# Cluster assignment of two attention halves through one bank and one argmax, with a reordered slot softmax and a new instruction order

## The chip, the cores and the metric

The kernel runs on one core of a Trainium2 chip. A core has TensorE (PE, which loads a stationary operand and streams a moving one against it), VectorE (DVE), ScalarE (ACT), GpSimd (POOL), and SyncE (SP), whose queue issues most of the DMAs. The metric is the device time of one launch in microseconds (us), taken as a median over runs.

## The reference

Two batches, eight heads, 768 tokens of 64 numbers. Each query and key token goes to the nearest of 16 centroids by a cosine, and a query attends only to keys of its own cluster. The result, 1536 tokens of 512, goes through a soft mixture of eight experts with four slots each, and then through a normed, gated feed-forward layer.

```python
q_assign = np.argmax(np.einsum('bhsd,hcd->bhsc', q_n, c_n), axis=-1)
k_assign = np.argmax(np.einsum('bhsd,hcd->bhsc', k_n, c_n), axis=-1)
mask = q_assign[:, :, :, None] == k_assign[:, :, None, :]
scores = np.where(mask, scale * np.matmul(q, k.transpose(0, 1, 3, 2)), -1e9)
x = softmax(scores) @ v                         # 1536 x 512
...
logits = x @ phi                                # 1536 x 32
slot_input = softmax(logits, axis=0).T @ x      # 32 x 512
slot_out[e] = np.maximum(slot_input[e] @ w1[e], 0.0) @ w2[e]    # 512 -> 1024 -> 512
y = softmax(logits, axis=1) @ slot_out          # 1536 x 512
...
xn = y / rms * rms_g
g = xn @ w_gate
out = (silu(g) * (xn @ w_val)) @ w_out          # 512 -> 1536 -> 512
```

## The kernel before

The program is written as operations (`Sched.op`), each with an engine or a choice of engines and a cost, the operations it depends on, and a sort key. A list scheduler in Python then fixes the order on every engine ahead of the build: of the operations whose inputs and buffers are free it takes the one with the least start time plus penalty. A table of constants at the head of the file (`KO`, an offset to the key for each operation's name, and some forty single numbers such as `SH`, `KS`, `AP`) feeds those keys and penalties. Buffers come from rings with fixed counts; `ms` is a ring of one PSUM bank, `big` one of three pairs of banks, `P` one of seven tiles in SBUF.

**Attention.** Eight pairs of heads, each made ready by `prepare(i)` and then worked off by two of the sixteen `unit`s. `prepare` loads q, k and v, and for each of the two halves of 384 tokens (`half(g)`) turns them on PE (L358), copies them to SBUF, multiplies them with the centroids (`cluster`, L395), copies the scores (`cevac`, tile cs), turns them again (`clusterT`, three transposes, L406) into a bank sc, adds the two partial scores of each (`part`, two reductions, L412) and finds the cluster with five passes of 192 numbers a partition (`argmax`, L436 to L445: maximum, difference, index where equal, maximum, one-hot E). Three transposes of E (`onehot`, L456) and three copies by ACT (`oq` L459, `ok` twice, L465) put the one-hot rows under q and k, where they act as the mask inside the score product. The chain of a half holds the one `ms` bank at several points, and it stands in DVE's queue among the score maxima of a unit.

A unit takes 768 keys by 768 queries in six blocks: `s1` (L526) multiplies scores once to find each row's maximum (`s1max`, DVE, L538), `mrow` puts the negated maxima (nr) where the second product can subtract them, `s2` (L578, L580) multiplies scores again, `exp` (ACT, L587) makes the weights P, `acc` (POOL or DVE, L242) adds the blocks of P for the sum, and `av` (L604) multiplies P with v. Then `lT` and `lgt` (L638, L644) make the sums and the slot logits, `oT` (L681) turns the output os. In the last unit the sums are made by `sums(0)` over acc and `sums(1)` over the last block of P (L661), in products whose moving operand is one column of ones.

**Slot softmax, experts, gates.** `middle` makes the slot softmax of the second batch: maximum (L1101 to L1110), exponentials, slot input si (L1181), its transposes (L1203, L1209) and the scaled slot input SITz (L1213), which the first expert product h (L1322) needs. The softmax of the other axis is `csm` (seven steps, L1233 to L1246, of which four on DVE come after the sum's exponential). The expert weights w come by SP's queue (L928, L930) in loads of 512 KB; the ring of w buffers comes free as the products h (L1322) and h2 (L1348) end. Of the loads in SP's queue one waits for the last logit sum L (L717). `cols` (L1363) turns an expert's result into columns of eight. Then `gates`: a Gram matrix (L1420), twelve products cq for the norm (L1448), the gate and value matrices of the 32 slots (gp, L1538), their casts and differences Gh and Gst (L234, L1571), the transposed slot weights cc (cT, L1291), and the loop over 36 blocks with g and v (L1652), the gate function sg (L1660), hh and hl, and the output products o (L1692). `warm` is a number of products that nobody reads (W3 to W8, WA0 to WA2, on PE).

## Time and profile before

| | us |
|---|---|
| runs: lowest, median, highest | 494.28, 494.79, 495.96 |
| profiled execution, its own time | 493.6 |
| span of the profile | 491.9 |
| PE busy | 456.6 (93%) |
| DVE busy | 321.7 (65%) |
| ACT busy | 279.2 (57%) |
| POOL busy | 216.5 (44%) |

The profile is of one execution. "Busy" counts the time in which an engine works on data. The clock column gives the share of full speed that PE's throttle granted, the two levels being 1.2 and 2.4 GHz (0.50 and 1.00). "Idle before" names what ended the idle time of an engine. By stage, the span is about: start to 36 us, attention to 292, slot softmax to 302, experts to 351, the way to the first gate product to 365, gates to 487, and a tail of output copies.

### The profile page before, as it was taken

To read this page: it belongs to the slowest core of one execution; us is meant where nothing else is said; L and a number is where in the kernel's file an instruction comes from. 1 tells how busy PE (TensorE), PEld (TensorE's weight loads), DVE (VectorE), ACT (ScalarE), POOL (GpSimd) and SP (SyncE) were. 2 spreads that over 40 slices of the span, in tenths; PEclk is the share of its full clock that TensorE was granted. 3 is DMA by queue.
4 is the path that set the end of the run, shared out by engine and by line. 5 is a ranking of instruction groups with operands and counts; after the bars stand their busy time and mean duration, and the time that the engine had idled before them with its cause. 6 is when DMAs were issued, how large, how long until landed. Compare 5 with 4: busy or idle time off the path is not lost. (4 is left out here: it accounts for less than half of the span.)

```text
span 491.9 us, 7819 instructions
## 1 busy us (share of the span) xinstructions
PE 456.6 (93%) x2794; PEld 330.3 (67%) x2794; DVE 321.7 (65%) x640; ACT 279.2 (57%) x582; POOL 216.5 (44%) x149
## 2 busy tenths in 40 slices
PE   6889998999999999899889998989989999999995
PEld 5766775777768756667667673335528878888884
DVE  6776889799999899788996143021157894444440
ACT  5568585876877866887756602231066664334332
POOL 2319767674877859484738800012025660000000
PEclk9889998999999999999999978999889999999999
DMA  6455415523634345746236949999502402002002
GB/s 173 117 154 171 115 41 151 135 65 97 198 112 150 94 134 171 200 155 190 98 121 227 339 170 362 378 398 392 225 0 90 168 1 87 0 1 85 0 1 85
DMA packets 30822, 71.96 MB, mean 146 GB/s; under 512 B 4064, under 2 KB 10304, under 8 KB 30784
## 3 DMA queue, kind: packets, MB, share of 16 engines
q1 hardware_dynamic: 26080, 55.73, 34.3%
q10 hardware_dynamic: 4704, 15.73, 10.1%
q8 instruction: 22, 0.36, 0.3%
q14 instruction: 16, 0.13, 0.1%
HBM read 61.97 MB, written 3.15 MB: 132 GB/s over the span
## 5 line engine op out<-in xcount | busy, mean ns | idle before, releaser
L242 POOL TENSOR_TENSOR acc<-acc,P 128x768 f32<-128x768 f32 x62 | 119.3, 1925 | 13.9 <-ACT P L587 10.5
L538 DVE TENSOR_REDUCE nm<-s 128x1 f32<-128x768 f32 x96 | 87.3, 948 | 12.5 <-PE s L526 12.0
L587 ACT ACTIVATE P<-s 128x768 f32<-128x768 f32 x96 | 75.3, 812 | 35.3 <-PE s L580 29.5
L1692 PE MATMUL o<-W,hh 128*128 128x512 f32 x288 | 89.9, 393 | 0.1
L578 PE MATMUL s<-q,k 128*128 128x384 f32 x192 | 70.0, 364 | 2.6 <-DVE nm L538 1.3
L604 PE MATMUL o<-P,rawv 128*64 128x384 f32 x384 | 67.8, 494 | 0.0
L580 PE MATMUL s<-q,k 97*128 97x384 f32 x192 | 65.7, 342 | 0.0
L1692 PEld LDWEIGHTS o<-W,hh 128*128 128x128 f32 x288 | 54.1, 188 | 12.5 <-POOL W L242 0.5
L526 PE MATMUL s<-k,q 96*128 96x384 f32 x192 | 52.4, 369 | 5.3 <-DVE nm L538 4.3
L1692 PE MATMUL o<-W,hl 128*128 128x512 f32 x144 | 56.6, 393 | 0.4 <-DVE hl L242 0.4
L242 POOL TENSOR_TENSOR acc<-P,P 128x768 f32<-128x768 f32 x16 | 30.0, 1875 | 46.3 <-ACT P L587 46.3
L578 PEld LDWEIGHTS s<-q,k 128*128 128x128 f32 x192 | 37.2, 194 | 11.4 <-DVE nm L538 3.4
L604 PEld LDWEIGHTS o<-P,rawv 128*64 128x64 f32 x384 | 25.3, 136 | 28.7 <-issue 27.2
L1664 DVE TENSOR_TENSOR hf<-v,sg 128x512 f32<-128x512 f32 x36 | 24.7, 689 | 28.6 <-ACT sg L1660 27.6
L526 PEld LDWEIGHTS s<-k,q 96*128 96x128 f32 x192 | 31.2, 190 | 16.1 <-DVE nm L538 9.9
L580 PEld LDWEIGHTS s<-q,k 97*128 97x128 f32 x192 | 37.2, 194 | 0.0
L1660 ACT ACTIVATE sg<-g 128x512 f32<-128x512 f32 x36 | 21.4, 597 | 27.7 <-PE g L1652 27.5
L234 ACT CAST hh<-hf 128x512 fp32r<-128x512 f32 x36 | 22.3, 621 | 21.9 <-DVE hf L1664 17.8
L242 DVE TENSOR_TENSOR hl<-hf,hh 128x512 fp32r<-128x512 f32 x29 | 21.2, 731 | 17.0 <-ACT hh L234 16.0
L1692 PEld LDWEIGHTS o<-W,hl 128*128 128x128 f32 x144 | 27.0, 188 | 6.9 <-DVE hl L242 0.8
L242 POOL TENSOR_TENSOR tokk<-rawk,tokk 128x384 fp32r<-128x384 f32 x15 | 16.4, 1092 | 33.3 <-DVE tokk L236 17.6
L676 ACT ACTIVATE pl<-pl 128x128 f32<-128x128 f32 x90 | 23.6, 262 | 7.8 <-PE pl L644 4.0
(261 smaller groups left out, 760.1 us busy)
## 6 DMA issues: line engine op xcount, KB each, us to landing
w<-in_moe_w_dram SPq DMA_DIRECT2D x56, 512.0 KB
gate<-in_moe_w_gate_dram ACTq DMA_DIRECT2D x12, 512.0 KB
val<-in_moe_w_val_dram ACTq DMA_DIRECT2D x12, 512.0 KB
out<-in_moe_w_out_dram SPq DMA_DIRECT2D x10, 512.0 KB
rawk<-in_k_dram SPq DMA_DIRECT2D x8, 384.0 KB
rawq<-in_q_dram SPq DMA_DIRECT2D x8, 384.0 KB
rawv<-in_v_dram SPq DMA_DIRECT2D x8, 384.0 KB
k<-k SPq DMA_DIRECT2D x16, 192.0 KB
```

Source lines behind the costliest of these rows:

```text
L234: nc.scalar.copy(out, in_)
L242: (nc.vector if e == "dve" else nc.gpsimd).tensor_tensor(out, a, b, op=op)
L526: nc.tensor.matmul(ps[:, g, :HQ], T[q2][0:96, h, qb : qb + 128], T[f"k2_{i}_{g}"][0:96, h, :], start=True, stop=True,)
L538: nc.vector.tensor_reduce(T[f"nm{u}"][:, n : n + 1], T[f"s1_{u}{h}{j}"][:, :, :HQ], op=ALU.max, axis=AX.XY, negate=True)
L578: nc.tensor.matmul(ps[:, h, :HQ], T[f"k1_{i}_{g}"][:, h, kb], T[q1][:, h, :], start=True, stop=False)
L580: nc.tensor.matmul(ps[:, h, :HQ], T[f"k2_{i}_{g}"][0:97, h, kb], T[q2][0:97, h, :], start=False, stop=True)
L587: nc.scalar.activation(p, T[f"s2_{u}_{c}"][:, :, :HQ], AF.Exp, scale=float(1.0 / D**0.5))
L604: nc.tensor.matmul(T[f"o{u}"][64 * h : 64 * h + 64, :HQ], T[f"rawv{i}"][:, h, c, :], T[f"P{u}_{c}"][:, h, :], start=(c == 0), stop=(c == N ...
L676: nc.scalar.activation(p, p, AF.Copy, accum_out=ls_()[:, h, j : j + 1])
L1660: nc.scalar.activation(self.tile(f"sg{tg}_{f}", [128, 512], F32, "sg", "outp", 2), T[f"g{tg}_{f}"], AF.Silu)
L1664: nc.vector.tensor_tensor(self.tile(f"hf{tg}_{f}", [128, 512], F32, "hf", "outp", 2), T[f"v{tg}_{f}"], T[f"sg{tg}_{f}"], op=ALU.mult)
L1692: nc.tensor.matmul(T[f"o{tg}{q}"], T[f"{x}{tg}_{f}"][:, ts], T[f"W{f // 6}"][:, w, f % 6, :], start=(f == 0 and n == 0), stop=(f == 11 and ...
```

## The change

It has five parts.

1. The two halves of a pair share one bank sc, one tile of copied scores cs and one argmax. Transposes and the two reductions of `part` are replaced by a product of cs with a constant `fold` (128 x 64, built once by one DVE reduction), which turns the scores and adds the parts in one go. `argmax` runs once a pair over 384 numbers a partition, `onehot` is one bank of six transposes, and six row copies on ACT follow in a row. The rings cs, csb and amb go; the first half's warm products at the start go too.
2. In unit 15 the sums are products with 64 equal columns of ones, `sums(1)` comes after the last av, and the row sums are read from two banks. All its `acc` run on DVE.
3. In `middle` the step of `csm` that follows the exponential comes after SITz is issued.
4. `cols` makes 64 columns (the same eight, eight times) rather than eight; eight warm products follow the last `cols` (W9), and the other warm counts grow (W3 6 to 9, W4 20 to 30, W5 3 to 8, W6 15 to 20, W8 6 to 10).
5. The table of constants is another one, so the order on every engine is another one.

```diff
-SH = 6.48
+SH = 7.03
...
-    "oT": -20.92, "s1": -0.82, "lT": 1.82, "split_hi": 67.65, "osb": 5.16, "mag": 19.15, "guard": 7.48,
+    "oT": -35.85, "s1": -0.08, "lT": 3.19, "split_hi": 83.82, "osb": 6.03, "mag": 31.37, "guard": 7.48,
...
-        cs=1, csb=1, am=1, amb=1, E=1, nm=2, nr=1, P=PR, acc=2, os=1, l=2,
+        am=1, E=1, nm=2, nr=1, P=PR, acc=2, os=1, l=2,
...
-            def clusterT(e):
-                pt = self.bank(f"sc{i}{g}", ms)
-                for j in range(3):
-                    at = slice(j * 128, (j + 1) * 128)
-                    nc.tensor.transpose(pt[:, 128 + j * 128 :][:, :128], T[f"cs{i}{g}"][:, at], K["id"])
-            def part(e):
-                pt = T[f"sc{i}{g}"]
-                for a, b in ((0, 128), (128, 192)):
-                    nc.vector.tensor_reduce(pt[:, a:b].rearrange("p (m c) -> p m c", c=C),
...
+        def both():
+            def clusterT(g):
+                def fn(e):
+                    if g == 0:
+                        self.bank(f"sc{i}")
+                    for j in range(3):
+                        nc.tensor.matmul(T[f"sc{i}"][:, 192 * g + 64 * j :][:, :64], T[f"cs{i}"][:, g, j * 128 : (j + 1) * 128],
+                                         K["fold"], start=True, stop=True)
+                return fn
+            CS = (cv[0], "P")
+            zg = z + DG
+            p = op({"pe": 700}, clusterT(0), key=zg - 10.25, alloc=("ms",), deps=cv, uses=[CS], after=self.lastE)
+            SC = (p, "ms")
+            p = op({"pe": 700}, clusterT(1), key=zg - 10.2, uses=[CS, SC])
...
-                    v = T[f"sc{i}{g}"][:, :192].rearrange("p (m c) -> p m c", c=C)
+                    v = T[f"sc{i}"][:, :384].rearrange("p (m c) -> p m c", c=C)
...
-            p = op({"pe": 200}, onehot, key=zg - 9, deps=[a], alloc=(ms,))
+            p = op({"pe": 400}, onehot, key=zg - 9, deps=[a], alloc=("ms",))
...
-                ac.append(op({"pool": 1885, "dve": (900, 900, AP)} if u < 15 or c < 4 else {"dve": 900}, acc(c), key=zu + c + 1.6,
+                ac.append(op({"pool": 1885, "dve": (900, 900, AP)} if u < 15 else {"dve": 900}, acc(c), key=zu + c + 1.6,
...
-                    nc.tensor.matmul(pt[:, 1, HQ + 64 + 2 * n + k : HQ + 65 + 2 * n + k], x, K["ones"], start=True, stop=True)
+                    nc.tensor.matmul(pt[:, k, 64 * n : 64 * n + 64], x, K["ones"].to_broadcast([128, 64]), start=True, stop=True)
...
-            pv[-1].after.append(op({"pe": 1340}, sums(1), key=ze - 10, uses=[(ex[-1], "P"), (p, "big")]))
+            last = op({"pe": 1340}, sums(1), key=ze - 10, uses=[(ex[-1], "P"), (p, "big")], after=pv[-1:])
...
+    K["fold"] = early.tile([128, 64], F32, name="fold_")
+    nc.vector.tensor_reduce(K["fold"].rearrange("p (m c) -> p m c", c=C),
+                            K["id"].rearrange("p (m t c) -> p m c t", t=2, c=C), op=ALU.add, axis=AX.X)
...
-            a = op({"act" if k == 2 else "dve": d}, csm(k), deps=[a], key=k0 + 2 + 0.1 * k)
+            a = op({"act" if k == 2 else "dve": d}, csm(k), deps=[a], key=k0 + 2 + 0.1 * k,
+                   after=[self.slots] if k == 3 else ())
...
-                    nc.tensor.matmul(ps[:, 8 * c : 8 * c + 8], T[f"H2s{ep}"][:, c * 128 : (c + 1) * 128],
-                                     T["F8"].rearrange("p x s -> p (x s)"), start=True, stop=True)
+                    nc.tensor.matmul(ps[:, 64 * c : 64 * c + 64].rearrange("p (r n) -> p r n", n=8), T[f"H2s{ep}"][:, c * 128 : (c + 1) * 128],
+                                     T["F8"].rearrange("p x s -> p (x s)").unsqueeze(1).to_broadcast([128, 8, 8]),
+                                     start=True, stop=True)
...
+            if ep == 3:
+                self.warm(W9, [c], kk + 6.17)
```

What the order does at three places. On PE, at the end of unit 15 (P_2 to P_5 are its last blocks of weights, o its output, acc the added blocks, os the copied halves of the output, phi the slot matrix, po a turned output), before:

```order
L604 MATMUL o_3333<-P_3_3310,rawv_2850 64x384 x2
L604 MATMUL o_3333<-P_4_3316,rawv_2850 64x384 x2
L661 MATMUL pl_3358<-ones,acc_3281 128x1 x6
L661 MATMUL pl_3358<-ones,P_5_3331 128x1 x6
L681 MATMUL po_3384<-idr,os_3288 128x128 x3
L604 MATMUL o_3333<-P_5_3331,rawv_2850 64x384 x2
L644 MATMUL pl_3358<-phi,os_3392 128x64 x3
L681 MATMUL po_3405<-idr,os_3392 128x128 x3
```

and after:

```order
L619 MATMUL o_3217<-P_2_3172,rawv_2746 64x384 x2
L675 MATMUL pl_3226<-ones,acc_3156 128x64 x6
L695 MATMUL po_3244<-idr,os_3165 128x128 x3
L619 MATMUL o_3217<-P_3_3182,rawv_2746 64x384 x2
L619 MATMUL o_3217<-P_4_3189,rawv_2746 64x384 x2
L619 MATMUL o_3217<-P_5_3206,rawv_2746 64x384 x2
L675 MATMUL pl_3226<-ones,P_5_3206 128x64 x6
L659 MATMUL pl_3226<-phi,os_3269 128x64 x3
L695 MATMUL po_3283<-idr,os_3269 128x128 x3
```

The sums over acc and the turning of the first os move ahead of the av products of P_3, and the sums over P_5 behind the last av products. So the last logits (phi, os) now come six products of sums after the av product that makes their os, and not right behind it.

On DVE, from the copy of the slot input SIs to the first work of the experts (L1233 to L1246 before are the steps of the other softmax; rd is the reciprocal of the slot sums), before:

```order
L236 COPY SIs<-si 128x256
L1233 TENSOR_REDUCE cm<-L 128x12
L1235 TENSOR_TENSOR Cx<-L,cm 128x384
L1171 TENSOR_SCALAR rd<-dsm 128x32
L1172 RECIPROCAL rd<-rd 128x32
L1240 TENSOR_REDUCE cs__3554<-Cx 128x12
L1242 TENSOR_SCALAR cs__3554<-cs__3554 128x12
L1244 RECIPROCAL cs__3554<-cs__3554 128x12
L1246 TENSOR_TENSOR Cx<-Cx,cs__3554 128x384
L1213 TENSOR_TENSOR SITz<-siT,rd 128x32x4
L1369 TENSOR_TENSOR SOg<-sc_3637,g 128x8x8
```

and after:

```order
L238 COPY SIs<-si 128x256
L1251 TENSOR_REDUCE cm<-L 128x12
L1253 TENSOR_TENSOR Cx<-L,cm 128x384
L1189 TENSOR_SCALAR rd<-dsm 128x32
L1190 RECIPROCAL rd<-rd 128x32
L1231 TENSOR_TENSOR SITz<-siT,rd 128x32x4
L1258 TENSOR_REDUCE cs__3456<-Cx 128x12
L1260 TENSOR_SCALAR cs__3456<-cs__3456 128x12
L1262 RECIPROCAL cs__3456<-cs__3456 128x12
L1264 TENSOR_TENSOR Cx<-Cx,cs__3456 128x384
L1389 TENSOR_TENSOR SOg<-sc_3536,g 128x8x8
```

SITz, which the first expert product needs, moves ahead of the four steps on cs and Cx.

On ACT, ahead of the gates (gp holds the gate and value matrices, Gh and Gst are their casts, cT the turned slot weights, sg the first gate function), before:

```order
L234 CAST cc_4069<-Cx 128x4x32
L234 CAST Gh<-gp_4027 64x512
L234 CAST cc_4069<-cT_4075 128x512
L234 CAST Gst<-gp_4027 64x512 x2
L234 CAST cc_4083<-cT_4093 128x512
L1660 ACTIVATE sg_0_4111<-g_0_4108 128x512
```

and after:

```order
L236 CAST cc_3982<-Cx 128x4x32
L236 CAST Gh<-gp_3940 64x512
L236 CAST Gst<-gp_3940 64x512 x2
L236 CAST cc_3982<-cT_3988 128x512
L976 ACTIVATE daout_2_4007<-out_2_3870 128x512
L1682 ACTIVATE sg_0_4018<-g_0_4001 128x512
```

The two casts Gst move ahead of the first copy of cT, and the second copy of cT leaves this place on ACT.

## Rows read from the trace of the kernel before

**Rows 1.** Stretches: start:end, length, busy us (count) PE PEld DVE ACT POOL, clock, DMA, GB/s.

```profile
60.00:260.00 200.00, 187.29 (x1167) 138.75 (x1166) 179.94 (x339) 146.66 (x332) 135.92 (x79) 0.99 0.45 132
...
288.00:294.00 6.00, 5.40 (x37) 4.41 (x33) 2.86 (x13) 0.48 (x1) 0.95 (x1) 0.51 0.14 42
...
302.00:349.00 47.00, 44.31 (x405) 18.54 (x406) 4.27 (x14) 9.38 (x19) 4.15 (x9) 0.97 1.02 387
...
349.00:352.00 3.00, 2.33 (x23) 2.06 (x22) 0.42 (x2) 0.59 (x1) 0.00 (x0) 1.00 0.70 280
...
352.00:359.00 7.00, 7.00 (x27) 3.99 (x28) 2.75 (x10) 1.64 (x3) 0.00 (x0) 0.57 0.01 4
...
365.00:487.00 122.00, 121.45 (x536) 95.95 (x534) 67.66 (x91) 60.34 (x103) 25.63 (x18) 1.00 0.13 45
```

**Rows 2.** PE's waits, 20 to 288: waiter <- releaser: us, times, longest.

```profile
PE s L526 <- DVE nm L538: 4.3, 12, 1.4
...
PE pe L456 <- DVE nr L236: 4.2, 4, 1.5
...
PE po L681 <- ACT k L465: 0.5, 2, 0.2
```

**Rows 3.** Groups by line: form, count | busy us, mean ns | idle before.

```profile
L412 DVE TENSOR_REDUCE sc<-sc 128x128 f32<-128x256 f32 (+1 forms) x32 | 11.6, 362 | 4.3 <-PE sc L406 2.8 <-ACT pl L676 0.8
...
L436 DVE TENSOR_REDUCE am<-sc 128x12 f32<-128x192 f32 x16 | 5.7, 355 | 0.5
...
L438 DVE TENSOR_TENSOR sc<-sc,am 128x192 f32<-128x192 f32 x16 | 5.9, 366 | 0.6
...
L1458 DVE TENSOR_TENSOR xq<-cq,Cx 128x384 f32<-128x384 f32 x1 | 0.6, 559 | 3.2 <-issue 3.2
```

**Rows 4.** PE in the attention: start us, us, line, tiles, form, count [idle before].

```profile
58.97 0.78 PE L644 MATMUL pl<-phi,os 128*128 128x64 f32 x6
...
59.56 0.60 PE L526 MATMUL s<-k,q 96*128 96x384 f32 x2
...
101.24 0.49 PE L406 MATMUL sc<-idr,cs 128*128 128x128 f32 x3
...
101.48 0.42 PE L578 MATMUL s<-q,k 128*128 128x384 f32 x1
```

**Rows 5.** PE at the end of unit 15: start us, us, as above.

```profile
281.03 3.45 PE L604 MATMUL o<-P,rawv 128*64 128x384 f32 x20
...
285.76 1.48 PE L661 MATMUL pl<-ones,P 128*128 128x1 f32 x12
...
287.56 0.99 PE L604 MATMUL o<-P,rawv 128*64 128x384 f32 x4
...
289.13 1.54 PE L644 MATMUL pl<-phi,os 128*128 128x64 f32 x6 [0.57 <-ACT os L234]
```

**Rows 6.** DVE from the last unit to the experts: start us, us, as above.

```profile
291.60 0.49 DVE L717 TENSOR_REDUCE L<-lx__3401 128x96 f32<-128x288 f32 x1
...
300.21 0.55 DVE L1240 TENSOR_REDUCE cs__3554<-Cx 128x12 f32<-128x384 f32 x1
...
301.75 0.28 DVE L1213 TENSOR_TENSOR SITz<-siT,rd 128x128 f32<-128x128 f32 x1
```

**Rows 7.** SP queue's waits, 268 to 352: waiter <- releaser: us, times, longest.

```profile
SPq L930 <- DVE L L717: 10.3, 1, 10.3
```

**Rows 8.** Busy time by stretch in the expert stage, columns as in Rows 1.

```profile
304.00:305.00 1.00, 1.00 (x11) 0.20 (x4) 0.00 (x0) 0.00 (x0) 0.00 (x0) 0.50 0.65 258
...
308.00:309.00 1.00, 1.00 (x12) 0.58 (x12) 0.00 (x0) 0.20 (x1) 0.00 (x0) 1.00 0.68 180
```

**Rows 9.** ACT ahead of the gates: start us, us, as in Rows 4.

```profile
362.18 0.59 ACT L234 CAST cc<-cT 128x512 fp32r<-128x512 f32 x1 [0.87 <-PE cT L1291]
...
362.66 1.17 ACT L234 CAST Gst<-gp 64x512 fp32r<-64x512 f32 x2
```

**Rows 10.** PE's first gate product: start us, us, as in Rows 4.

```profile
364.70 0.47 PE L1652 MATMUL g<-cc,Gst 128*128 128x512 f32 x1 [1.42 <-DVE Gst L1571]
```

More of the change, by code (lines that the diff above doesn't have):

```diff
@@ new lines @@
+    "socs": 77.85, "fold": 12.4, "fsi": -20.16, "fz": 38.25, "qlo": -29.2, "drec": 148.45, "mv": -49.27,
+    "linv": -67.97, "xrow": -89.71, "exp": -0.46, "trans": -3.66, "mrow": -126.03, "oq": -81.14, "sums": -109.82,
+    "tok": 8.0, "ok": 6.63, "centroids_": 142.06, "cols": -58.06, "csm": -92.42, "ds": 12.02, "dsum": -46.87,
+    "fes": -103.2, "four": -9.43, "h1": 72.42, "h2": -11.23, "hT": -1.12, "hTe": -79.15, "hf": -34.9, "high": -30.06,
+    "lgt": -33.39, "lgx": -160.62, "lgx0": -53.94, "load": 96.77, "mb": 31.73, "mm": 17.24, "mp1": -46.24, "mpT": 5.51,
@@ L491, in prepare @@
         half(1)
+        both()
         return O
@@ L756, in unit @@
         x = op({"dve": (960, 960, LP), "act": 1650} if u < 15 else {"dve": 200}, lsum,
[L757 removed]
+               key=ze + (2.1 if u < 15 else -10), deps=[last] if u == 15 else (), uses=[PL])
         zl = ze if u < 15 else ze - 12
```

157 lines of the change are left out of this document (77 added, 80 removed), and 3 rows, old and new, of the table KO.

## The prediction

> **What bounds the kernel now.** Read the stretches first [rows 1]. In the attention PE works 187.29 of 200 us at a clock of 0.99 and DVE 179.94, so PE is the bound there, with 12.71 us of holes, and DVE, with 20.06 us of idle time, is close behind. In the expert stage DMA is busy throughout (share 1.02, 387 GB/s), so the end of that stage is set by when the loads begin and by whether they ever pause. From 365 on PE works 121.45 of 122 us at full clock; only its start can move. Two stretches stand out by their clock: 288 to 294, where last sums and logits are made at 0.51, and 352 to 359, where PE is busy 7.00 of 7.00 us at 0.57. Next come PE's waits [rows 2]: in the attention it waits most for the row maxima (L538, 4.3 us in 12 times) and for the copy of negated maxima nr (4.2 us in 4), both work in DVE's queue. Then the groups [rows 3], which give the prices of what is removed, and the timelines [rows 4, 5, 6, 9, 10], which give prices of what is added and the steps between stages.
>
> The profiled execution took 493.6 us, the runs a median of 494.79; the sum below is made against 493.6, and 1.2 is added at the end.
>
> **Attention: DVE's relief.** A half has two reductions at 362 ns and five passes of 192 numbers, of which the reduction took 355 and the product with a broadcast 366 [rows 3]; the other three lie near these. With 0.36 for each that is 0.72 + 1.80 = 2.52, and 5.04 a pair. After, a pair has five passes of 384 numbers. The one such operation on a PSUM operand in the trace took 559 ns [rows 3]: 2.80 a pair. DVE saves 2.24 a pair, about 18 us in eight. The edits of the order that shift copies between DVE, ACT and POOL nearly cancel in number, and I cost them at nothing.
>
> On this point the Trainium skill, in "VectorE: DVE Perf Modes", the section on the TRN2 errata, says that each instruction pays a fixed cost, and gives 120 cycles plus one per element at 0.96 GHz for a PSUM source; an estimate by it is 325 ns for 192 and 525 for 384, so that ten short passes against five long ones would save 0.62 a pair where the rows give 3.60 - 2.80 = 0.80. The trace's 366 and 559 agree in kind and lie 34 to 41 ns above the page; by the page, DVE's relief would be 16.7 us in eight pairs.
>
> What is the relief worth? PE is the bound, so only its holes can shrink. A span of 200 us holds some 6.2 pairs, so DVE's load there falls by 13.9 us, from 179.94 to 166.0, and its idle time rises from 20.06 to 34.0. If a wait for a queue goes as the inverse of the idle time behind it, the holes shrink to 20.06 / 34.0 = 0.59 of themselves: 12.71 x 0.41 = 5.2 us. The bounds are 0 (the holes are waits for operations themselves) and 12.7 (all gone). That the nr copies wait behind argmax passes in DVE's queue speaks for a share; that no more than 8.5 us name DVE in the two large rows [rows 2] speaks against all.
>
> **Attention: PE's price.** Three transposes (x3) run from 101.24 to 101.48, when the next product starts: 0.24. Three f32 products of 64 columns (x6, two passes each) run from 58.97 to 59.56: 0.59 [rows 4]. The fold's products have that shape, so a half pays 0.35 more. Two halves and seven pairs (the first pair is in the startup) are 14 x 0.35 = +4.9 on the engine that is the bound. One-hot transposes and centroid products stay in number. Both bounds: 0, if all of it falls into holes, and +4.9.
>
> The Trainium skill, in "TensorE: Matmul & The Clock Gate", section Terms, speaks against this edit: transpose mode is four times faster for FP32 than a plain product. By that a 64-column product would cost twice a 128-column transpose, 0.48 for three and +3.4 in all as an estimate; the rows' ratio of 0.59 to 0.24 is 2.5, and decides.
>
> Body: +4.9 - 5.2 = **-0.3**. The row copies on ACT now come six in a row rather than three; PE waits for one of them twice today, 0.5 in all [rows 2], and I cost the burst at nothing while ACT, busy 146.66 of 200 [rows 1], has room.
>
> **Startup.** The first pair's chain is shorter by 2.2 us for both halves together, but its first half must now wait for the second, at most that one's own 2.52. I take **0**, bounds -2.2 and +2.5.
>
> **End of unit 15.** Before, the last av products (0.99 for four) made os, ACT copied it while PE idled for 0.57, and the logits took 1.54, with the clock at 0.51 [rows 1, 5]. After, the sums over P_5 stand between, so the 0.57 goes. The same logits took 0.78 in the body [rows 4]: -0.76, if the clock stays. Four av products out of twenty in 3.45 would be 0.69: -0.30. The sums in 64 columns cost 2 x 0.59 = 1.18 against 1.48 in one column [rows 4, 5]: -0.30. I cost the sums over acc at nothing in their new place, since twelve av products still stand ahead of them and cover DVE's last acc. Sum **-1.9**; with the clock falling as before only -0.6 is sure. The engine was busy on one-column products right before the clock fell; now they are 64 wide, which is why I take full clock. SP's queue waited 10.3 us for L [rows 7], which ended at 291.60 + 0.49 = 292.09 [rows 6]. The loads restart when it does, the stage behind is bound by DMA, so this gain goes through to the end. The bounds are 0 and -2.5.
>
> **Slot softmax and experts.** Four passes from 300.21 to 301.75 stand ahead of SITz [rows 6]; it now goes first, so the experts start some 1.5 us earlier, and the 1.9 on top. The stage ends with the DMAs, so this pays only where loads pause for buffers that PE holds: two stretches of 1 us at shares of 0.65 and 0.68 [rows 8] lose 0.35 + 0.32 = **-0.7** (bounds 0 and -0.7). The four passes then run beside expert products, where DVE is busy 4.27 of 47 us [rows 1]; nothing waits for them there. The larger warm counts of this stage fill PE's waits for the softmax, and I cost them at nothing, as I do the new order of SP's loads, which are the same in number.
>
> **Gates.** From 352 to 359 PE worked 7.00 us at 0.57 [rows 1]; at full clock the same work takes 4.0: -3.0. Before the fall PE had products of eight columns and was busy 2.33 of 3.00 us [rows 1]; now cols are 64 wide, with eight warm products behind. A pass of one column takes 1.48 / 12 = 0.12 [rows 5], one of 64 columns 0.59 / 6 = 0.10 [rows 4], so the width costs nothing; the eight warm products, at 0.12 some 1.0, lie in the 0.67 of holes, and I neglect the 0.3 that may stick out. Then the first gate product waited 1.42 for Gst's difference on DVE [rows 10], for which the two casts (1.17) stood behind a cast of cc on ACT [rows 9]. The casts now come first, and 1.4 goes; next is cc's cast, on ACT right after. Sum **-4.4**, bounds -1.4 (clock falls) and -4.4; nothing else holds the 121.45 us after it.
>
> Sum: -0.3 + 0 - 1.9 - 0.7 - 4.4 = -7.3, so 486.3 profiled, **487.5** at the median.
>
> **Rivals.**
> - *The clock falls all the same.* The products of the gates' norm stay 32 columns wide. Then -0.3 - 0.6 - 0.7 - 1.4 = -3.0: 491.8.
> - *The restart of the loads isn't ahead.* If another buffer holds SP's queue, the end of unit 15 and the pauses give nothing: -0.3 - 4.4 = -4.7, 490.1. For it speaks that the queue has many waits; against it, that the 10.3 us is the long one [rows 7].
> - *The holes nearly vanish.* Three quarters of 12.71 go, 9.5: body -4.6, sum -11.6, 483.2. One onehot wait per pair rather than two speaks for it.
> - *Slower: the body pays in full.* A pair's first half waits for its second, one `ms` bank is held from the first fold product to the one-hot, and six ACT copies in a row stand ahead of an exp. If the holes don't shrink, the fold costs its 4.9, and with one wait of 0.2 as in [rows 2] for each of seven pairs 1.4 more: +6.3. With the clock falling too: +6.3 - 0.6 - 0.7 - 1.4 = +3.6, 498.4. It comes out slower by over 0.3% (1.5 us) once the body costs over 4.2 at a falling clock, or 8.5 without.
>
> **How the numbers follow.** Chances: forecast 0.45, clock 0.15, restart 0.10, holes 0.12, slower body 0.18. 0.3% of 494.8 is 1.5 us, about what a measurement can tell from no change. Faster by more: the first four less 0.03 of their upper edges, 0.79. Within: these 0.03 and 0.07 of the body's near side, 0.10. Slower: 0.11. The range reaches down below 483.2 by 1.7, for a startup that gains, and up to 494.5, which leaves out most of the slower body: 481.5 to 494.5.
>
> **What the changed profile would show.** Right: five argmax passes near 0.56 and no reduction before them; the fold's three products 0.59 a half; PE's waits for L538 and nr under 5 us together; clock 1.00 from 284 to 292 and through the norm's products; no wait of the last logits for os; L near 290; SITz ahead of the csm passes; the first gate product by some 6 us earlier with no wait for Gst. Wrong: a clock near 0.5 in these places, PE's holes in the body at 12 us or more, PE waiting for ACT's row copies, or a restart of the loads after 291.

## The result and the profile after

The changed kernel took 487.14 us in the median of four runs (486.22 to 489.62), against 495.2 (494.28 to 495.96) for the kernel before: a ratio of 0.984, with a 95% interval of 0.980 to 0.988. That is 8.1 us less, where 7.3 were forecast, and the time lies in the forecast range. On a second occasion it took 489.63 in the median of four (485.42 to 491.47), and the kernel before 495.2 in seven runs there (492.52 to 499.49): 5.6 less. The eight runs of both occasions have a median of 488.3, with which the kernels below are compared. Most of those ran on two later occasions, on which the kernel before took 496.3 (25 runs, 491.42 to 500.57) and 497.2 (13 runs, 493.3 to 498.64) and the changed kernel was not run, so that a difference from 488.3 may be off by a microsecond or two. Small differences between kernels can therefore not be read from their times; they are read from their stages.

The profile of the changed kernel is of an execution of 489.62 us, one of the longer ones, while that of the kernel before was of a short one (493.6). The two profiles differ by 4.0 us, not by 8; for such a pair the prediction's own sum was 7.3 (486.3).

The page, first lines:

```profile
span 487.8 us, 7889 instructions
...
PE 455.8 (93%) x2857; PEld 333.2 (68%) x2857; DVE 303.7 (62%) x564; ACT 277.1 (57%) x590; POOL 205.8 (42%) x146
```

The stretches, as in [rows 1] (start:end, length, busy us and count for PE, PEld, DVE, ACT, POOL, then clock, DMA share and GB/s):

```profile
60.00:260.00 200.00, 192.16 (x1225) 144.88 (x1225) 167.95 (x285) 147.54 (x340) 132.21 (x80) 0.98 0.46 135
...
288.00:294.00 6.00, 5.29 (x75) 4.96 (x73) 3.55 (x15) 0.36 (x2) 0.00 (x0) 1.00 0.63 219
...
299.00:345.00 46.00, 43.03 (x403) 18.42 (x404) 6.17 (x19) 10.21 (x21) 3.75 (x8) 1.00 1.03 391
...
346.00:349.00 3.00, 2.88 (x32) 2.55 (x29) 0.42 (x2) 0.40 (x1) 0.00 (x0) 1.00 0.60 238
...
349.00:352.00 3.00, 3.00 (x19) 1.76 (x20) 0.81 (x3) 0.19 (x1) 0.00 (x0) 0.92 0.00 1
...
352.00:357.00 5.00, 5.00 (x22) 1.32 (x19) 3.05 (x11) 2.92 (x6) 0.50 (x1) 0.70 0.00 0
```

In the attention PE is now busy 192.16 of 200 us and DVE 167.95: PE's holes went from 12.71 to 7.84, and DVE's idle time from 20.06 to 32.05. Where last sums and logits are made, the clock was 0.51 and is 1.00; DMA moved 42 GB/s there and now moves 219. The loads now restart ahead of L: in the 10 us that end with L, DMA moved 179 GB/s before and moves 266 now. In the expert stage DMA is as busy as before. Ahead of the gates the clock still falls, but later: 0.92 in 349 to 352, 0.70 in 352 to 357.

The two large waits of [rows 2], in the same stretch of the span (waiter, releaser, us in all, times, longest):

```profile
PE pe L465 <- DVE nr L238: 2.9, 4, 0.8
...
PE s L541 <- DVE nm L553: 2.1, 4, 1.4
```

The argmax passes, and the fold on PE (groups as in [rows 3], timeline as in [rows 4]):

```profile
L445 DVE TENSOR_REDUCE am<-sc 128x24 f32<-128x384 f32 x8 | 4.4, 550 | 5.6 <-PE sc L422 5.5
...
L447 DVE TENSOR_TENSOR sc<-sc,am 128x384 f32<-128x384 f32 x8 | 4.5, 567 | 0.8
...
L454 DVE TENSOR_TENSOR E<-sc,am 128x384 bf16<-128x384 f32 x8 | 4.5, 557 | 0.3
```

```profile
70.49 0.78 PE L422 MATMUL sc<-fold__133,cs 128*128 128x64 f32 x6
...
71.08 0.60 PE L541 MATMUL s<-k,q 96*128 96x384 f32 x2
```

Five passes cost 550 to 567 ns each, for the 560 that were assumed; three products of the fold take from 70.49 to 71.08, 0.59 us, as assumed. The Trainium skill, in "VectorE: DVE Perf Modes", the section on the TRN2 errata, has a row for a PSUM source from which an estimate for such a pass is 525 ns: the measured passes lie 5 to 8% above it, and the measurement decides.

The end of unit 15 on PE, then L and SITz on DVE, and the waits of SP's queue (compare [rows 5 to 7]):

```profile
284.61 2.16 PE L619 MATMUL o<-P,rawv 128*64 128x384 f32 x12
...
286.69 1.55 PE L675 MATMUL pl<-ones,P 128*128 128x64 f32 x12
...
288.08 0.83 PE L659 MATMUL pl<-phi,os 128*128 128x64 f32 x6
```

```profile
290.06 0.49 DVE L731 TENSOR_REDUCE L<-lx__3271 128x96 f32<-128x288 f32 x1
...
298.76 0.29 DVE L1231 TENSOR_TENSOR SITz<-siT,rd 128x128 f32<-128x128 f32 x1 [0.20 <-DVE rd L1190]
```

```profile
SPq L948 <- PE pl L675: 6.9, 1, 6.9
...
SPq L948 <- DVE L L731: 1.9, 1, 1.9
```

No wait stands ahead of the last logits, which take 0.83 us and not 1.54. L ends at 290.55 and SITz comes at 298.76, against 292.09 and 301.75. In SP's queue one load waits for the sums and the next only 1.9 us for L, where one load had waited 10.3.

The gates: the norm's products, the gate matrices and the first gate product on PE, then ACT and DVE (compare [rows 9, 10]):

```profile
349.96 1.51 PE L1470 MATMUL cq<-Q,cc 128*128 128x32 f32 x12
...
351.40 5.49 PE L1560 MATMUL gp<-wgv,SOg 128*64 128x512 f32 x20
...
359.33 0.47 PE L1674 MATMUL g<-cc,Gst 128*128 128x512 f32 x1 [1.99 <-DVE Gst L1593]
...
359.97 1.07 PE L1560 MATMUL gp<-wgv,SOg 128*32 128x512 f32 x8
```

```profile
355.94 0.58 ACT L236 CAST Gh<-gp 64x512 fp32r<-64x512 f32 x1 [1.07 <-PE gp L1560]
...
356.55 0.58 ACT L236 CAST Gst<-gp 64x512 fp32r<-64x512 f32 x1
...
357.89 0.58 ACT L236 CAST Gst<-gp 64x512 fp32r<-64x512 f32 x1 [0.76 <-DVE Gst L1593]
...
357.16 0.69 DVE L1593 TENSOR_TENSOR Gst<-gp,Gh 64x512 fp32r<-64x512 f32 x1 [1.56 <-ACT Gst L236]
...
358.50 0.69 DVE L1593 TENSOR_TENSOR Gst<-gp,Gst 64x512 fp32r<-64x512 f32 x1 [0.65 <-ACT Gst L236]
```

Before, PE's lines at this place were (cT are turned products, the gate matrices end where the first of them starts):

```profile
353.31 2.74 PE L1448 MATMUL cq<-Q,cc 128*128 128x32 f32 x12
355.98 5.69 PE L1538 MATMUL gp<-wgv,SOg 128*64 128x512 f32 x20
361.60 0.54 PE L1291 MATMUL cT<-idr,cc 128*128 128x128 f32 x4
```

The norm's products take 1.5 (the next product starts at 351.40) and not 2.74. PE's wait for Gst is longer than before, 1.99 for 1.42, but it also begins earlier: eight more turned products stood ahead of it before and stand behind the first gate product now. From the end of the gate matrices to the first gate product it took 3.1 us before and takes 2.5. On ACT and DVE the casts and the differences now follow each other one by one.

Stage by stage, with the second profile of the changed kernel beside the first. Each line goes from the end named above it to its own:

| Stage, up to | forecast | before | after, two profiles | change |
|---|---|---|---|---|
| end of the last exponential | -0.3 | 280.73 | 280.41, 280.57 | -0.3, -0.2 |
| end of L | -1.9 | 11.36 | 10.14, 10.13 | -1.2, -1.2 |
| end of the last expert product | -0.7 | 56.92 | 55.17, 55.15 | -1.8, -1.8 |
| first gate product | -4.4 | 15.69 | 13.61, 12.56 | -2.1, -3.1 |
| end of the span | 0 | 127.20 | 128.47, 129.69 | +1.3, +2.5 |

The sum is -4.1 and -3.8. What the medians show beyond that (8.1 on the first occasion, 5.6 on the second) is not in these profiles.

The profiles of the experiments below tell how firm these lines are, since each experiment leaves most stages as they are. In the order of the kernel before, the one without its two reductions repeats the lines behind the last exponential within 0.4 us (11.23, 57.33, 15.68, 127.17). In the order of the changed kernel, the last exponential ends at 279.7 to 281.6 wherever the attention was left alone, though the first one starts at 38.4 to 41.7. From L to the last expert product it takes 54.6 to 56.2 in the six profiles whose unit 15 and slot softmax were left alone, so that the gain of this line is 0.7 to 2.4. To the first gate product it takes 12.56 in every later profile in which the gates were left alone, and 13.61 in the first alone.

### The profile page after: what moved, and what is told of

It is laid out like the page before. It is cut to its first block, busy times and chain, and to the rows that moved or that the text cites. A ratio compares the mean times of both kernels' runs of the same rounds, so it can differ in the third digit from the quotient of the medians.

```text
span 487.8 us, 7889 instructions
## 1 busy us (share of the span) xinstructions
PE 455.8 (93%) x2857; PEld 333.2 (68%) x2857; DVE 303.7 (62%) x564; ACT 277.1 (57%) x590; POOL 205.8 (42%) x146
## 4 chain that ended last, share of the span: by engine, by line
PE 76%; DVE 13%; DMA 5%; issue 3%; ACT 2%; POOL 0%; ACTq 0%; DVEq 0%; POOLq 0%
PE o L1714 19%; PE o L619 14%; PE s L593 6%; PE s L595 5%; PE s L541 5%; DVE nm L553 5%; DMA w<-in_moe_w_dram 4%; PE pc L397 2%; PE h L1367 2%; PE g L1674 2%; PE gp L1560 2%; PE v L1674 2%; PE sc L422 2%; PE h L1341 2%; PE ptk L360 2%
## 5 line engine op out<-in xcount | busy, mean ns | idle before, releaser
L244 POOL TENSOR_TENSOR acc<-acc,P 128x768 f32<-128x768 f32 x60 | 114.7, 1911 | 24.1 <-ACT P L602 20.0
L553 DVE TENSOR_REDUCE nm<-s 128x1 f32<-128x768 f32 x96 | 88.7, 952 | 24.4 <-PE s L541 24.0
L619 PE MATMUL o<-P,rawv 128*64 128x384 f32 x384 | 70.9, 512 | 0.0
L593 PE MATMUL s<-q,k 128*128 128x384 f32 x192 | 68.8, 358 | 0.9 <-DVE nm L553 0.5
L244 DVE TENSOR_TENSOR hl<-hf,hh 128x512 fp32r<-128x512 f32 x27 | 19.6, 726 | 43.3 <-ACT hh L236 29.9
L244 POOL TENSOR_TENSOR acc<-P,P 128x768 f32<-128x768 f32 x15 | 27.5, 1831 | 37.5 <-ACT P L602 37.5
L236 ACT COPY os<-o 128x384 f32<-128x384 f32 (+1 forms) x28 | 14.7, 525 | 20.2 <-PE o L1714 7.1
```

What stands on the lines that cost most here:

```text
L236: nc.scalar.copy(out, in_)
L244: (nc.vector if e == "dve" else nc.gpsimd).tensor_tensor(out, a, b, op=op)
L553: nc.vector.tensor_reduce(T[f"nm{u}"][:, n : n + 1], T[f"s1_{u}{h}{j}"][:, :, :HQ], op=ALU.max, axis=AX.XY, negate=True)
L593: nc.tensor.matmul(ps[:, h, :HQ], T[f"k1_{i}_{g}"][:, h, kb], T[q1][:, h, :], start=True, stop=False)
L619: nc.tensor.matmul(T[f"o{u}"][64 * h : 64 * h + 64, :HQ], T[f"rawv{i}"][:, h, c, :], T[f"P{u}_{c}"][:, h, :], start=(c == 0), stop=(c == N ...
```

## The experiments

Theory: the body of the attention comes out even, since DVE's relief pays for the fold, and the gain is made behind it by the sums of unit 15, the earlier loads and a clock that stays up. Rivals: the merged argmax is the gain; the order alone is the gain; the clock does something else.

**The changed kernel again.**

> The changed kernel as it is, once more. The profile at hand is of an execution of 489.62 us, 2.5 above the median of 487.14; what it loses should stand in the startup (first exponential at 38.3 against 36.0 before). If that loss belongs to the execution, another profile with a time near 487 shows the first exponential near 36 and every later stage as far behind it as before; if it belongs to the kernel, the first exponential stays at 38 and another stage is shorter.

Median 489.63 of four. The execution that was profiled took 489.93 and had its first exponential at 40.72, later than the 38.35 of the first profile, and yet its last one ended at 280.57, within 0.2 of the other. So the start of the first exponential is not what sets the end of the body, and the expectation that a short execution would show a short startup could not be tried. From the last exponential to the last expert product the stages repeat within 0.1 us. At the gates the two differ: here the clock held during the gate matrices,

```profile
350.08 1.51 PE L1470 MATMUL cq<-Q,cc 128*128 128x32 f32 x12
...
351.53 3.79 PE L1560 MATMUL gp<-wgv,SOg 128*64 128x512 f32 x20
...
358.41 0.47 PE L1674 MATMUL g<-cc,Gst 128*128 128x512 f32 x1 [2.36 <-DVE Gst L1593]
...
359.04 1.91 PE L1560 MATMUL gp<-wgv,SOg 128*32 128x512 f32 x8
```

which took 3.98 us (351.53 to 355.51) rather than 5.42, and the gate products after the wait were slow instead (eight of them 1.91 us for the 1.07 in the first profile). At the first output product the two profiles stand 19.0 and 19.2 us after the last expert product, where the kernel before stood at 20.4. In the five other profiles with the same gates (of experiments below) the clock held during the gate matrices each time. In three of them the products after the wait were slow again, and the first output product came after 19.1 to 20.4 us; in two, the fold twice and SITz behind the four passes, they ran at full clock too, here with the fold twice,

```profile
366.64 1.06 PE L1560 MATMUL gp<-wgv,SOg 128*32 128x512 f32 x8
```

and it came after 17.95. So where the clock falls, and whether it does, differs from execution to execution.

**One part alone, by code or by table.**

Three kernels: the changed one with the halves apart again,

```diff
-            p = op({"pe": 700}, clusterT(0), key=zg - 10.25, alloc=("ms",), deps=cv, uses=[CS], after=self.lastE)
+            p = op({"pe": 335}, clusterT, key=zg - 10.2, alloc=(ms,), uses=[(x, cst)], after=self.lastE if ms == "ms" else ())
...
+            p = op({"dve": 640}, part, key=zg - 9.9, uses=[SC])
...
```

the kernel before with the new table, and the changed code with the old one:

```diff
-SH = 6.48
+SH = 7.03
...
-W4 = 20
+W4 = 30
...
```

> The changed kernel with its first part undone: three transposes, two reductions and five passes for each half again, all else and the table kept. My theory (the relief of DVE just pays for the fold's 4.9 us on PE): within 1.5 us of the changed kernel, 486 to 489. Rival one (the merged argmax is where the gain came from): 490.5 or more. Rival two (the fold costs more than it gives): 485.5 or less.

> The kernel before with the new table of constants and warm counts, and no other edit. My theory (the code of the last unit, of the slot softmax and of cols gives the larger part): 491 to 494. Rival (the order alone is the gain): 489 or less.

> The changed code with the table and the warm counts of the kernel before. My theory (code gives the larger part of the 8 us): 488.5 to 491.5. Rival (the order alone is the gain): 493 or more; it can also be slower than the kernel before, since that table was made for other operations.

They took 536.9, 539.4 and 528.6 us in the median: 33 to 44 slower than the kernel before, far above every figure that was expected (the rivals' "490.5 or more" and "493 or more" hold by their wording alone). PE waits in other places there, as in the first of them:

```profile
PE po L682 <- DVE E L447: 5.9, 2, 3.0
...
PE s L580 <- DVE k L238: 4.2, 2, 2.7
```

The order differs throughout the attention: in the first of them some 880 of PE's 2857 instructions stand in another place than in the changed kernel. The table was fitted to one set of operations and costs, and with another set the same keys give another order. Why these orders cost so much is not shown. So these runs don't tell what a part is worth, and no part of the gain can be credited to code or table by them. Only their stages behind the attention serve below. From here on every experiment keeps the order of the engines, and changes what an instruction does or one place.

**DVE's work of before, in the new order.** The reductions and short passes are put back, the order of the other engines is that of the changed kernel word for word.

```diff
+                    if k == 0:
+                        sc = T[f"sc{i}"]
+                        for g in range(2):
+                            for a, b in ((0, 128), (128, 192)):
+                                nc.vector.tensor_reduce(sc[:, 384 : 384 + (b - a) // 1].rearrange("p (m c) -> p m c", c=C)[:, : (b - a) // C],
+                                                        sc[:, 0 : 2 * (b - a)].rearrange("p (m t c) -> p m c t", t=2, c=C),
+                                                        op=ALU.add, axis=AX.X)
+                    for g in range(2):
+                        h, w = slice(12 * g, 12 * g + 12), slice(3 * g, 3 * g + 3)
...
-                        nc.vector.tensor_reduce(mx, v, op=ALU.max, axis=AX.X)
+                            nc.vector.tensor_reduce(mx[:, h], v[:, h], op=ALU.max, axis=AX.X)
...
```

> The changed kernel in its own order on every engine, with DVE's work of the kernel before put back: ten passes of 192 numbers a pair for five of 384, and four reductions a pair of the removed sizes whose results nobody reads. DVE gets 2.24 us a pair back, 18 in all. My theory (the relief is worth about 5 us of PE's holes in the body): 3 to 7 us above the changed kernel, and PE's idle time between 60 and 260 back at 11 to 13 us from 7.8. Rival one (PE is the bound, DVE's load matters little): less than 2 us above. Rival two (the argmax chain and its queue set the time): 9 us or more above.

506.11 us, 17.8 above the 488.3 of the changed kernel (and 9.8 above the kernel before on the same occasion), for 18 us of DVE work. The last exponential ends at 297.89, 17.3 later than in the second profile of the changed kernel; 4.8 of it is there at the first exponential (45.52). PE, from 60 to 260:

```profile
60.00:260.00 200.00, 184.86 (x1179) 140.01 (x1178) 172.70 (x323) 143.24 (x329) 127.98 (x80) 0.99 0.46 132
```

In the second profile of the changed kernel that line read:

```profile
60.00:260.00 200.00, 192.65 (x1240) 146.61 (x1238) 169.48 (x286) 149.04 (x343) 133.72 (x81) 0.99 0.47 135
```

PE's holes are 15.1 us, up from 7.4, though DVE is idle for 27.3 of 200. In that stretch PE now waits for E, the argmax's last pass, where the changed kernel shows no such wait (pm are the turned row maxima):

```profile
PE pm L579 <- DVE E L464: 5.6, 6, 1.2
```

The number is the second rival's: with these orders, 18 us of argmax cost 17.3. Two things the run does not tell. All of the added work lies inside the argmax, so a fuller queue of DVE and a longer way from the fold to the one-hot rows come together. And the order was fitted to the short argmax, so what it costs to lengthen it need not be what shortening it gained.

**The fold twice.**

```diff
-                    for j in range(3):
+                    for j in (0, 1, 2, 0, 1, 2):
```

> The changed kernel in its own order, with each product of the fold made twice: 0.59 us more PE work a half, 16 halves, 9.4 us in all, 8.3 of them in the body. My theory (PE is the bound of the attention, so the fold's price is paid in full): 7 to 10 us above the changed kernel, with PE's idle time from 60 to 260 about as in the changed kernel. Rival (the fold's products fall into holes): 0 to 4 us above, and the holes shrink.

496.66 us in ten runs, 8.3 above; the last exponential ends at 287.45, 6.9 later. PE from 60 to 260 is busy 2.1 us more than in the second profile of the changed kernel:

```profile
60.00:260.00 200.00, 194.76 (x1273) 150.21 (x1269) 159.66 (x280) 146.21 (x339) 131.10 (x79) 0.98 0.47 135
```

The price of the fold is paid for the larger part (6.9 of 9.4 by the end of the body), as forecast. That PE's idle time would stay as it was is not what came: it is 5.2 us, for 7.4 and 7.8, so some of the added work fell into holes, as the rival said.

**Less DVE work, in the old order.** The kernel before without its two reductions of each half (so it finds other clusters).

```diff
             def part(e):
-                pt = T[f"sc{i}{g}"]
-                for a, b in ((0, 128), (128, 192)):
...
+                pass
...
-                    v = T[f"sc{i}{g}"][:, :192].rearrange("p (m c) -> p m c", c=C)
+                    v = T[f"sc{i}{g}"][:, 128:320].rearrange("p (m c) -> p m c", c=C)
```

> The kernel before in its own order, without the two reductions of each half that add the partial scores (left out, so the clusters are other ones): 0.72 us a half less on DVE, 11.6 in all. By the step of the prediction (holes shrink as the inverse of DVE's idle time): idle time of DVE from 20 to 29 us in 200, PE's holes from 12.7 to 9, some 3.5 to 5 us faster than the kernel before. Rival one (DVE's queue sets the time one to one, as putting the work back into the changed kernel suggests with 17 us for 18): 9 to 12 faster. Rival two (the old order hides this work): less than 2 faster.

490.54 us (487.9 to 493.06), 4.8 to 6.6 less than the 495.35 and 497.18 of the kernel before on that occasion. Its profile (491.01) shows less, 2.6 against that of 493.6: the first exponential at 34.09, 1.9 sooner than before, and the last one ends at 277.88, 2.9 sooner. So 1.9 is startup, and 1.0 is the body:

```profile
60.00:260.00 200.00, 187.97 (x1169) 140.85 (x1167) 170.01 (x316) 146.22 (x333) 136.11 (x80) 0.98 0.45 134
```

DVE is down by 9.93 us, its idle time up to 29.99, and PE's holes are 12.03 where the inverse law asked for 8.5. Of the waits, that for nr is gone, and others have grown:

```profile
PE s L522 <- DVE nm L534: 6.1, 13, 1.5
...
PE fsi L1041 <- ACT fE L1032: 2.9, 1, 2.9
```

Between these two profiles the old order hides this work in the body, as the second rival says. The time of the whole moved by what the theory said or somewhat more, and not by under 2. Since the profile of the kernel before is of a short execution, the other 2 to 4 us are placed in no stage, and the body can hold some of them.

**The sums of unit 15 as before.** The orders of all engines are those of the changed kernel up to this place.

```diff
-                    nc.tensor.matmul(pt[:, k, 64 * n : 64 * n + 64], x, K["ones"].to_broadcast([128, 64]), start=True, stop=True)
+                    nc.tensor.matmul(pt[:, 1, HQ + 64 + 2 * n + k : HQ + 65 + 2 * n + k], x, K["ones"], start=True, stop=True)
...
-            last = op({"pe": 1340}, sums(1), key=ze - 10, uses=[(ex[-1], "P"), (p, "big")], after=pv[-1:])
+            pv[-1].after.append(op({"pe": 1340}, sums(1), key=ze - 10, uses=[(ex[-1], "P"), (p, "big")]))
```

> The changed kernel with its second part undone: products of one column, the last av products behind the sums over P_5, and acc partly on POOL. The orders of all engines are those of the changed kernel up to this place. My theory (the idle time for os goes and the clock stays up): from the end of the last exponential to the end of the last logit sum L it takes 1.2 to 2 us longer, with PE's clock near 0.5 in 288 to 294 and 0.6 us of PE waiting for os; the loads restart later by as much. Rival (the clock falls for another reason, not the narrow columns): the clock stays near 1.0 there and the step is 0.6 longer at most.

491.75 us in ten runs, 3.4 above the changed kernel. From the last exponential to L it takes 10.89 rather than 10.13, and from L to the first expert product 10.41 rather than 8.57, because the clock stays low well into the slot softmax:

```profile
288.00:294.00 6.00, 5.43 (x37) 4.49 (x37) 2.48 (x10) 0.48 (x1) 0.95 (x1) 0.54 0.41 126
```

The last logits took 1.54 after 0.57 of waiting for os again. The last expert product is 2.0 later behind the last exponential. So the part works as said; its first step (0.8) is smaller than forecast, and a second one of 1.8 in the slot softmax was not in the sum. How much the first step is worth depends on when the clock falls: the kernel before under the new table has the same one-column sums and a wait of 0.58, but its last logits took 0.88, only the thirty warm products behind them were slow (3.23), and L came 10.03 us after the last exponential. The edit undoes the width, the place of the sums and the place of acc together; which of the first two, or the wait for os that follows from them, brings the fall is not told apart.

**Narrow cols, no warm products behind them.**

```diff
-                    nc.tensor.matmul(ps[:, 64 * c : 64 * c + 64].rearrange("p (r n) -> p r n", n=8), T[f"H2s{ep}"][:, c * 128 : (c + 1) * 128],
-                                     T["F8"].rearrange("p x s -> p (x s)").unsqueeze(1).to_broadcast([128, 8, 8]),
-                                     start=True, stop=True)
+                    nc.tensor.matmul(ps[:, 64 * c : 64 * c + 8], T[f"H2s{ep}"][:, c * 128 : (c + 1) * 128],
+                                     T["F8"].rearrange("p x s -> p (x s)"), start=True, stop=True)
...
-W9 = 8
+W9 = 0
```

> The changed kernel with its fourth part undone: cols of eight columns and no warm products behind the last of them; the other warm counts stay. My theory (the width and the warm products hold the clock until the norm's products are over): the clock falls to 0.5 some 1.5 us sooner after the last h2, the twelve norm products take 2.5 or more rather than 1.5, and the first gate product comes 1 to 2 us later. Rival (the other warm counts do that): the norm's products take 1.5 again and the first gate product comes within 0.4.

492.67 us in ten runs, 4.3 above. From the last expert product to the first gate product it takes 15.11, against 13.61 and 12.56; the norm's products take 2.74 again, and the clock is as low as it was in the kernel before. From 345 to 360 it is 0.77; in the 14 us behind the last expert product it is 0.76 in both, against 0.88 and 0.97 in the two profiles of the changed kernel:

```profile
345.00:360.00 15.00, 13.24 (x67) 6.98 (x65) 5.09 (x17) 4.52 (x10) 0.50 (x1) 0.77 0.18 71
```

Theory, not rival: it is the width and the eight products that put off the fall of the clock. The kernel before under the new table, which has the other warm counts but neither of these two, agrees: 2.75 for the norm's products, 15.11 from the last expert product to the first gate product. Which of the two does it is not told apart. What is left of the gain without them, 15.69 to 15.11, is 0.6, which the casts' new place and the rest of the order share.

**SITz behind the four passes.**

```diff
-            a = op({"act" if k == 2 else "dve": d}, csm(k), deps=[a], key=k0 + 2 + 0.1 * k,
-                   after=[self.slots] if k == 3 else ())
+            a = op({"act" if k == 2 else "dve": d}, csm(k), deps=[a], key=k0 + 2 + 0.1 * k)
...
+        self.slots.after = [a]
```

> The changed kernel with SITz behind the four passes of the other softmax on DVE, all else and the order of the other engines kept. My theory (the expert stage is bound by DMA, an earlier start pays only for the pauses): from L to the first expert product 1.5 us more, from there to the last expert product 0.8 to 1.5 less, so 0 to 0.7 later in all. Rival (the start of the experts counts in full): the last expert product comes 1.5 later.

From L to the first expert product it takes 9.99, 1.4 more; from there to the last 46.94, 0.4 more and not 0.8 to 1.5 less (where this step was not touched it takes 46.0 to 47.6). The start of the experts counts in full, as the rival says. DMA's share in the first 8 us of this stage fits that, here:

```profile
300.00:302.00 2.00, 2.00 (x15) 0.42 (x13) 0.00 (x0) 0.00 (x0) 0.00 (x0) 0.59 0.68 268
...
302.00:304.00 2.00, 2.00 (x16) 0.57 (x12) 0.00 (x0) 0.00 (x0) 0.00 (x0) 0.56 0.87 268
...
304.00:306.00 2.00, 2.00 (x21) 0.42 (x13) 0.00 (x0) 0.60 (x1) 0.00 (x0) 1.00 0.71 240
...
306.00:308.00 2.00, 2.00 (x24) 0.89 (x24) 0.00 (x0) 0.59 (x1) 0.00 (x0) 1.00 0.84 332
```

and in the changed kernel:

```profile
300.00:302.00 2.00, 2.00 (x24) 0.64 (x20) 0.56 (x1) 0.23 (x2) 0.00 (x0) 1.00 0.98 371
...
302.00:304.00 2.00, 2.00 (x20) 0.68 (x12) 0.00 (x0) 0.60 (x1) 0.00 (x0) 1.00 0.93 334
...
304.00:306.00 2.00, 2.00 (x22) 0.63 (x24) 0.00 (x0) 0.58 (x1) 0.00 (x0) 1.00 0.98 371
...
306.00:308.00 2.00, 2.00 (x24) 0.52 (x16) 0.00 (x0) 0.00 (x0) 0.00 (x0) 1.00 1.03 418
```

With shares of 0.68, 0.87, 0.71 and 0.84 the loads lose 1.8 us in these 8, against 0.2 there: they wait for buffers that the first expert products hold, and these run at a clock of 0.59 and 0.56 in the first 4 us, after PE's longer wait for SITz. How much is the wait and how much the clock isn't told apart. The median, 489.09 of four, can't show 1.8 us. PE's order differs in one more place, at 330 us, where sixteen products trade places with a group of warm ones. (Without the ordering edge of the change the program comes out the same under the new table: it is the table that puts SITz first, and the edge does nothing here.)

**Two additions.**

```diff
-                self.tile("Gst", [128, 2 * FF], F32R, None, "outp")
+                for b in range(6):
+                    self.tile(f"Gst{b}", [128, 512], F32R, None, "outp")
...
             self.lastT = [p]
+            if i == 0:
+                self.warm(30, [p], -15.5)
```

> The changed kernel with two additions: the stacked gate matrix Gst lies in six tiles rather than one, so that its four writers don't wait for each other's halves of other blocks, and thirty warm products follow the first pair's fold, where PE is idle for 3.1 us waiting for the argmax. My theory: PE's wait for Gst of 2.0 to 2.4 shrinks by 0.7, the clock stays at 1.00 between 16 and 26, and the first exponential comes up to 1.5 sooner; 0.7 to 2 us faster than the changed kernel. Rival (the wait for Gst comes from the cast's place on ACT, the startup's end from DVE): no change in either stage.

489.57 us (483.54 to 493.55), not to be told from the changed kernel. PE still waits 2.4 for Gst, so the shared tile is not what makes the writers follow each other; what does (the bank gp, which all four read, is a candidate) stays open. The profile is of a long execution (493.55). There the warm products fill PE's hole, but at the low clock,

```profile
16.00:20.00 4.00, 4.00 (x33) 4.00 (x33) 2.17 (x4) 0.00 (x0) 0.00 (x0) 0.50 0.28 97
```

and the first exponential came at 41.36. In this execution neither addition helps; whether the warm products would in another is not shown.

**The kernel before again.**

> The kernel before, as it is, for a second profile on another occasion. By the theory that the profile of 493.6 us is of a short execution, its stages repeat within 0.3 us from the last exponential to the first gate product, and what differs stands in the startup and the body. If the stages behind the body differ, comparing one profile of each kernel isn't enough.

495.35 us in ten runs (491.94 to 502.19). The profile caught one of the longest (501.02). Its body took 249.5 us against 244.8, and behind the body two stages did not repeat within 0.3: the experts took 0.8 longer, the way to the first gate product 1.6. By the expectation's own words, one profile of each kernel isn't enough, and a profile of so long an execution does not settle which stage holds the part of the gain that the others don't show. Behind the body the kernel without two reductions is the better witness for the first profile, which it repeats within 0.4.

## Why the prediction was right, and where not

The time was right (487.5 for 487.1 to 488.3) and so was the sign. That it was so close is in part luck: the sum of five terms made 7.3 against a profile of 493.6, where the profiles after show 4.1 and 3.8, and the terms' errors cancel in part. The medians moved by 8.1 and 5.6, and no run says where the part beyond 4 lies.

- **Startup and body: right in sum, wrong in mechanism.** Forecast -0.3 and 0, measured -0.3 and -0.2 together. But the first exponential came 2.4 and 4.8 later, at the startup's bound of +2.5 and beyond it, and from the first to the last exponential it took 2.7 and 4.9 less (244.8 before, 242.1 and 239.9 after). The end of the body did not follow the startup in any profile of this order whose attention was left alone; why, and why the startup is longer, is open. The prices of the single operations were right: 0.56 a pass, 0.59 for three products, and PE's holes went down by 4.9 for 5.2. What failed is the step "a wait for a queue goes as the inverse of the idle time behind it". In the old order DVE's idle time rose to 30 us and the holes moved by 0.7, not by 4; in the new order giving DVE 18 us back cost 17.3, not 3 to 7. What a load on DVE costs PE depends on where the order has put the work. So that the holes fell by nearly the forecast amount is luck, and how much of it is the relief and how much the new order is not shown.
- **End of unit 15: mechanism right, size smaller.** The wait for os went, the logits took 0.83, the clock stayed at 1.00. The step to L gave 1.2 of 1.9: of the sum's four terms the wait gave 0.6 and the logits 0.7, as forecast; the av products 0.2 for 0.3; and the sums in 64 columns nothing, since twelve products took 1.39 us to the next start (1.35 in one column) where 1.18 was put. Behind the logits L came 0.2 later. The loads did not restart with L, as the prediction had it, but some 2 us ahead of it, one of them released by the sums. And a clock held up here also serves the slot softmax: with the part undone, 1.8 more behind L.
- **Expert loads: under-sized.** Forecast -0.7 from two stretches of 1 us; from L to the last expert product it was -1.8. The prediction let an earlier first expert product pay only for those two pauses. Moving SITz alone made 1.4 of start, and the later stage did not win it back: the loads, which had started earlier, then paused 1.8 us in 8 rather than 0.2. But the loads' own restart ahead of L is in this line too, 0.9 MB more by the end of L (179 and 266 GB/s over 10 us), over 2 us at the 390 GB/s of this stage; how the 1.8 divides between the two is not shown.
- **Gates: over-sized.** Forecast -4.4, of which the clock was to give 3.0. That part was sound: the norm's products took 1.51 for 2.74, and with the gate matrices at full clock 2.9 came, in all profiles but the first (1.4). What the sum lacks is that the clock can fall later: in five of seven profiles it did. Of the 1.4 for Gst only 0.2 to 0.6 came: ahead of Gst stood not only ACT's cast of cc, which the forecast read, but writers of Gst that take turns, 0.58 and 0.69 us each, and the second cast waits for a difference on DVE. And the prediction's "nothing else holds the 121.45 us after it" was wrong: eight turned products of cT (1.1 us), which stood ahead of the first gate product, stand now behind it, with a new wait of 0.6 for hf, so that of 2.1 to 3.1 the last stage gives 1.3 to 2.5 back.
- **The slower side.** PE waits neither for ACT's burst of row copies nor for the merged halves beyond the startup (3.1 us once, for the first pair). The body did not pay in full, since the holes shrank. But with DVE's old work in the new order the kernel is 9.8 us slower than the kernel before, so the new order without the shorter argmax would have been a loss.

One figure beside the sum was added up wrongly: DVE's relief by the second way of pricing, 16.7 us, is 16.5 from its own numbers (8 x (0.62 + 1.44)). Nothing hangs on it.

What stays open: where the medians' gain beyond the 4 us of the profiles lies. Single executions of either kernel spread over 6 to 10 us, and no profile shows the kernel before near its median.

## What to carry to other kernels

Where a scheduler's table sets the order, code and table are one thing: each of them alone cost 33 to 44 us here. To learn what an edit is worth, keep the order and change what one instruction does; to forecast it, don't scale holes by an engine's idle time, but ask for each wait where its releaser stands in its queue. And where a transfer-bound stage begins with full buffers, as here, ask when its first consumer starts: 1.4 us there counted in full.

## What the runs showed of the hardware

A low clock lasted beyond the work before it: after twelve products of one column (1.40 us) and a wait of 0.57, the clock was 0.54 over 288 to 294 with PE busy 5.43 of 6 us, thirty warm products among it at 3.41 us for 1.84. And putting off a fall can move it rather than take it away: with the gate matrices spared (3.98 for 5.42), the products after the next wait of 2.36 were slow, and the first output product came no sooner than where they had been slow themselves (19.2 and 19.0 us). Programs with the same gates also ran this stretch with no fall at all (two of seven profiles, 17.95 us to the first output product for 19.0 to 20.4).
